# Queries and keys loaded on both halves of the partitions, and a step of its own for the store of x, in a kernel of block-causal attention, Fourier mixing and feed-forward

## The chip, the core and the metric

The kernel runs on one core of one Trainium2 chip. A core has five engines that work side by side and meet through semaphores: TensorE (PE; its weight loads are shown as PEld), VectorE (DVE), ScalarE (ACT), GpSimd (POOL) and SyncE (SP), which here only issues transfers. Each engine executes its own instructions in the order in which they were written; an instruction that waits holds up everything behind it on the same engine. Transfers run on 16 DMA engines. Data lies in SBUF, on 128 partitions; PE writes to PSUM. The metric is the time of one execution in microseconds, and lower is better.

## The reference

```python
# q, k, v: (8, 8, 576, 64), i.e. batch, heads, sequence, head dimension
scores = np.matmul(q, k.transpose(0, 1, 3, 2)) / np.sqrt(D)
mask = block_i >= block_j                      # blocks of 64 positions
attn = softmax(np.where(mask, scores, -1e9))   # in float32
x = np.matmul(attn, v)                         # put together to (8, 576, 512)
mixed = np.real(fft(fft(x, axis=1), axis=2))
u = x + mixed
un = (u - mean(u)) / np.sqrt(var(u) + 1e-6)    # over the last axis
out = u + np.maximum(un @ w_ch1, 0.0) @ w_ch2  # 512 -> 2048 -> 512
```

There are 8 batches of 8 heads, so 64 heads in all, numbered 0 to 63 here. All of it is asked for in float32.

## The kernel before

**One loop writes the whole order.** The kernel is cut into steps (the class Step, line 144): a function that writes instructions, its time on PE, a chain of later costs ("D0.95" is 0.95 us on DVE, "A" is ACT, "G" is POOL, "Q" is the DMA queue of SP, "L" is a latency that takes no engine), the keys it comes after, and a place. Lanes of steps (lines 363 to 502 and 904) each yield their steps in order. The loop at line 914 keeps a clock of its own by these costs: it issues, among the steps at the head of the lanes, the one with the lowest place that is due by that clock, and where none is due it puts in a step of the feed-forward matmuls (the filler) or of the preparation of the weights. So the order on each engine is fixed before the kernel runs, from estimates. Matmuls are kept in that order (line 202); the scheduler of the language below it may still shift instructions of the other engines against each other.

**One head.** Queries and keys come as one array of 64 rows (the head dimension) by 1152 columns (576 of q, then 576 of k). load_head (line 311) loads them to raw. A score is to have nearly float32 accuracy from matmuls in a format of fewer bits (fp32r), so q and k are each split into a leading part and a rest, and three of the four products are added up in PSUM. lead (line 316) rounds both on ACT (a cast of 64 x 1152) into LEAD, on partitions 0 to 63; below these, four rows hold the mask. REST (128 partitions) takes four quarters: in its q columns the rest of q on partitions 0 to 63 and a copy of the lead of q on 64 to 127; in its k columns a copy of the lead of k on 0 to 63 and the rest of k on 64 to 127. The two copies are transfers inside SBUF (lead_copies, line 319, lines 321 and 322), the rests are differences, one on DVE (line 328), one on POOL (line 330). So one matmul of REST with itself gives q_rest k_lead + q_lead k_rest, one of LEAD with itself q_lead k_lead and the mask (lines 404 and 405).

Each score group of a head (three groups of rows, n = 0, 1, 2; the first has four matmul pairs, the others one) goes from PSUM through the maximum (DVE, line 411), two exponentials (ACT, line 425, in f16 and f32), their difference (POOL, line 426), and a transpose by DMA from SP's queue (turn, line 430). PE then multiplies with V (values, line 435), and DVE divides by the sum (lines 463 to 467) into the tile x, which holds a pair of heads in one buffer. After the second head of a pair two transfers on SP's queue write x to a buffer in HBM (lines 471 and 474); they are written right behind the division, in the same step as the value matmuls.

LEAD, REST, raw and the probabilities have two buffers each, so head h reuses those of head h - 2. The planner lets the cast of head h start when the exponentials of head h - 2 are due (line 373), the scores when the copies (key TC, line 375) and both differences (T2) are due (line 483).

**After eight heads** a batch's x is read back from HBM in two orders (mirror, line 517, due when the last values of the batch are), transformed by matmuls, normalized, and fed to the feed-forward matmuls. Only batch 0 runs beside the loading and splitting of the weights (lines 793 to 876); heads of later batches are let in when the loading steps are written (line 922).

## Time and profile before

| what | value |
|---|---|
| time, median of 3 runs | 1315.21 us (1314.83 to 1320.55) |
| the profiled execution | 1318.01 us, its span 1316.2 us |
| mean granted clock of PE in it | 0.966 |
| instructions of PE, DVE, ACT, POOL | 9620, 1697, 1329, 715 |
| DMA traffic | 161.77 MB, mean 123 GB/s |
| transposes on SP's queue | 192 (three for each head) |

The profiled execution is one execution, taken by the hardware profiler. The span runs from its first instruction to its last. Views of it are used as follows: the page gives the busy time of each engine and its share of the span; the stretches give the same for parts of the span; the waits say which engine stood idle at which line and what ended that wait, summed up; the time order lists single instructions with start and duration; the groups put instructions of the same line, operation and shape together. A wait that hung on several semaphores is put down to the one that came last by the profile, which can be the wrong one.

### The profile page before, as it was taken

How to read it: one execution, taken by the hardware profiler on the slowest of the kernel's cores; microseconds unless marked ns; L12 is line 12 of the kernel's file. 1: busy time of each engine (PE TensorE's matmuls, PEld its weight loads, DVE VectorE, ACT ScalarE, POOL GpSimd, SP SyncE). 2: the span in 40 equal slices, each digit the busy share in tenths (PEclk: the TensorE clock that was granted, in tenths of full speed). 3: DMA queues.
4: the chain of work that ended last, by engine and by line, in shares of the span. 5: the costliest groups of instructions: out<-in, count | busy, mean ns of one | idle time of the engine just before them, and what ended most of it. 6: DMA issues, size and time to landing. Idle time of an engine off the chain costs nothing.

```text
span 1316.2 us, 25240 instructions
## 1 busy us (share of the span) xinstructions
PE 1125.2 (85%) x9620; PEld 826.4 (63%) x9620; DVE 713.2 (54%) x1697; ACT 620.6 (47%) x1329; POOL 549.0 (42%) x715
## 2 busy tenths in 40 slices
PE   1344175798989898989999999999999999999998
PEld 1244154575767676667767677667667767767665
DVE  7954477646465755576656656674673432412211
ACT  3645747764456543655666545665562211111110
POOL 2635725554455553536655366645741500300000
PEclk9999986798999998999999999999999999999999
DMA  9999607987568745765898567985863000000000
GB/s 320 230 203 237 176 5 141 163 172 151 96 148 152 172 85 130 144 152 116 173 193 165 108 120 191 173 167 114 172 119 82 26 16 17 21 1 17 16 17 16
DMA packets 307178, 161.77 MB, mean 123 GB/s; under 512 B 259281, under 2 KB 277857, under 8 KB 306929
## 3 DMA queue, kind: packets, MB, share of 16 engines
q1 hardware_dynamic: 300416, 135.94, 51.1%
q10 hardware_dynamic: 4384, 16.78, 3.9%
q0 software_dynamic: 2256, 7.45, 1.8%
q8 instruction: 75, 1.23, 0.4%
q14 instruction: 47, 0.38, 0.1%
HBM read 58.37 MB, written 18.87 MB: 59 GB/s over the span
## 4 chain that ended last, share of the span: by engine, by line
PE 52%; DVE 9%; DMA 8%; POOL 3%; issue 3%; ACT 2%; SPq 0%; DVEq 0%; POOLq 0%; ACTq 0%
PE h L202 20%; PE acc L202 20%; PE ps L202 8%; DMA turn<-prob 6%; PE av L202 3%; DVE M L411 2%; DMA u<-xd,rows 1%; DVE rest L328 1%; DVE tmp L541 1%; POOL prob L426 1%; PE ps L205 1%; ACT prob L425 1%; POOL rest L330 1%; ACT p L425 1%; DVE tmp L542 1%
## 5 line engine op out<-in xcount | busy, mean ns | idle before, releaser
L202 PE MATMUL h<-uh,W 128*128 128x256 f16 x2304 | 424.7, 276 | 0.0
L426 POOL TENSOR_TENSOR prob<-p,prob 128x288 f16<-128x288 f32 (+4 forms) x384 | 286.9, 754 | 276.2 <-ACT p L425 259.4
L202 PEld LDWEIGHTS <-W 128*128 128x128 f16 x3456 | 332.9, 99 | 67.1 <-issue 4.7
L202 PE MATMUL acc<-W,gh 128*128 128x512 f16 x1152 | 348.4, 384 | 0.0
L202 PE MATMUL h<-ul,W 128*128 128x256 f16 x1152 | 317.5, 276 | 0.0
L425 ACT ACTIVATE prob<-ps,M 128x64 f16<-128x64 f32 (+2 forms) x358 | 164.6, 493 | 138.6 <-DVE M L416 137.3
L742 DVE SCALAR_TENSOR_TENSOR gl<-h,gh 128x512 f16<-128x512 f32 x144 | 99.0, 687 | 238.6 <-ACT gh L741 238.2
L202 PE MATMUL acc<-W,gl 128*128 128x512 f16 x576 | 220.7, 383 | 1.1 <-DVE gl L742 0.6
L202 PE MATMUL av<-VH,turn 128*128 128x65 f16 x1920 | 130.7, 205 | 96.9 <-DMA turn<-prob 82.2
L741 ACT ACTIVATE gh<-h 128x512 f16<-128x512 f32 x144 | 86.7, 602 | 269.0 <-PE h L202 268.4
L202 PEld LDWEIGHTS <-turn 128*128 128x128 f16 x2880 | 116.9, 105 | 126.0 <-DMA turn<-prob 98.7
L411 DVE TENSOR_REDUCE M<-ps 128x1 f32<-128x288 f32 (+2 forms) x358 | 138.8, 426 | 88.1 <-PE ps L202 72.5
L425 ACT ACTIVATE p<-ps,M 128x64 f32<-128x64 f32 (+2 forms) x358 | 171.1, 494 | 15.1 <-POOL prob L426 12.5
L202 PEld LDWEIGHTS <-gh 128*128 128x128 f16 x1152 | 105.7, 100 | 97.1 <-issue 9.9
L330 POOL TENSOR_TENSOR rest<-raw,lead 64x576 fp32r<-64x576 f32 x64 | 106.9, 1671 | 115.7 <-ACT lead L317 89.4
L202 PE MATMUL ps<-rest 128*128 128x288 f32 (+2 forms) x358 | 123.7, 363 | 34.2 <-ACT p L425 26.6
L202 PE MATMUL av<-VL,turn 128*128 128x64 f16 x960 | 118.6, 204 | 0.0
L202 PEld LDWEIGHTS ps<-rest 128*128 128x128 f32 x358 | 73.8, 206 | 47.2 <-ACT p L425 32.3
L202 PE MATMUL ps<-lead 68*128 68x288 f32 (+2 forms) x358 | 103.3, 322 | 0.0
L202 PEld LDWEIGHTS <-gl 128*128 128x128 f16 x576 | 56.9, 99 | 71.5 <-issue 2.7
L317 ACT CAST lead<-raw 64x1152 fp32r<-64x1152 f32 x64 | 73.5, 1149 | 18.6 <-PE ps L202 18.4
L202 PEld LDWEIGHTS ps<-lead 68*128 68x128 f32 x358 | 74.3, 208 | 1.3
(166 smaller groups left out, 1197.2 us busy)
## 6 DMA issues: line engine op xcount, KB each, us to landing
raw<-in_qk_dram SPq DMA_DIRECT2D x64, 288.0 KB
rest<-lead SPq DMA_DIRECT2D x128, 144.0 KB
W<-in_moe_w_ch_dram ACTq DMA_DIRECT2D x14, 1024.0 KB
V<-in_v_dram SPq DMA_DIRECT2D x32, 320.0 KB
xd<-x SPq DMA_DIRECT2D x32, 256.0 KB
out_dram<-u SPq DMA_DIRECT2D x32, 256.0 KB
u<-xd SPq DMA_DIRECT2D x8, 512.0 KB
turn<-prob SPq DMA_TRANSPOSE x192
```

The source lines that it names most:

```text
L202: return tc.keep_in_program_order(nc.tensor.matmul(*args, **kw))
L205: return tc.keep_in_program_order(nc.tensor.transpose(*args, **kw))
L317: nc.scalar.copy(LEAD[h % NB][0:D, 64:], raws[h])
L328: nc.vector.tensor_tensor(x0[0:D, 64:64 + S], raw[:, 0:S], x1[0:D, 64:64 + S], op=ALU.subtract)
L330: nc.gpsimd.tensor_tensor(x0[D:P, 64 + S:], raw[:, S:], x1[0:D, 64 + S:], op=ALU.subtract)
L411: nc.vector.tensor_reduce(m[:, i:i + 1], x, axis=AX.X, op=ALU.max)
L425: nc.scalar.activation(to, x, AF.Exp, bias=bias[:, c:c + 1], scale=0.125)
L426: nc.gpsimd.tensor_tensor(pl, p32, ph, op=ALU.subtract)
L541: nc.vector.tensor_tensor(e[0:r], X[c][0:r], U[c][0:r], op=op)
L542: nc.vector.tensor_tensor(e[0:r, 1:256], e[0:r, 1:256], e[0:r, 511:256:-1], op=op)
L741: nc.scalar.activation(gh, t, AF.Relu)
L742: nc.vector.scalar_tensor_tensor(gl, t, 0.0, gh, op0=ALU.max, op1=ALU.subtract)
```

## The change

The array of queries and keys is doubled before the launch: its 64 rows come twice, so that raw has 128 partitions, both halves with the same data. The cast now fills all of ONE (the former REST): lead of q and of k on both halves. DVE then overwrites the q columns of the upper half with the rest of q, so ONE times ONE gives q_lead k_lead + q_rest k_lead. TWO (the former LEAD, with the mask rows) gets the lead of q by a new copy on DVE (lead_q, straight from raw into the fp32r tile) and the rest of k by POOL's difference; TWO times TWO gives q_lead k_rest and the mask. The two transfers inside SBUF are gone. In the planner the step that was "Q1.2", "L2.2" behind the cast is "D0.6" behind the load.

The two stores of a pair of x leave the values function and become store_x, issued by a lane of its own (store_lane) with place 2g + 1.6, due when the values of the pair are, with a cost of 1.1 us on SP's queue. The mirror of a batch now comes after the last of these steps, and the last value step of later heads asks for the store step of the pair before.

```diff
--- before.py
+++ after.py
@@ -229,8 +229,8 @@
 
 
     NB = 2
-    LEAD = [const.tile([KM, 64 + 2 * S], F32R, name=f"lead{i}") for i in range(NB)]
-    REST = [const.tile([P, 64 + 2 * S], F32R, name=f"rest{i}") for i in range(NB)]
+    TWO = [const.tile([KM, 64 + 2 * S], F32R, name=f"two{i}") for i in range(NB)]
+    ONE = [const.tile([P, 64 + 2 * S], F32R, name=f"one{i}") for i in range(NB)]
     PROB = [[const.tile([P, 2, w], F16, name=f"prob{i}_{x}") for i, w in enumerate(WIDTHS)] for x in range(2)]
     TURN = [const.tile([P, 2 * w // P, P], F16, name=f"turn{i}") for i, w in enumerate(WIDTHS)]
     DEN = [const.tile([P, 5], F32, name=f"DEN_{i}") for i in range(2)]
@@ -238,9 +238,9 @@
     VL = [const.tile([P, 5, 2, D], F16, name=f"VL_{i}") for i in range(2)]
     ZT = const.tile([34, NCOS], F32R, name="ZT")
     for i in range(NB):
-        nc.gpsimd.dma_start(LEAD[i][D:KM], c_masks)
-        nc.vector.tensor_scalar(LEAD[i][0:D, 0:64], ones[0:D, 0:64], 0.0, None, op0=ALU.mult)
-        nc.vector.tensor_scalar(REST[i][:, 0:64], ones[:, 0:64], 0.0, None, op0=ALU.mult)
+        nc.gpsimd.dma_start(TWO[i][D:KM], c_masks)
+        nc.vector.tensor_scalar(TWO[i][0:D, 0:64], ones[0:D, 0:64], 0.0, None, op0=ALU.mult)
+        nc.vector.tensor_scalar(ONE[i][:, 0:64], ones[:, 0:64], 0.0, None, op0=ALU.mult)
     for n, blocks in enumerate(BLOCKS):
         for j, at in blocks:
             for prob in PROB:
@@ -310,24 +310,24 @@
 
     def load_head(h):
 
-        raws[h] = work.tile([D, 2 * S], F32, name="raw", bufs=2)
+        raws[h] = work.tile([P, 2 * S], F32, name="raw", bufs=2)
         nc.sync.dma_start(raws[h], qk[h])
 
+
+
     def lead(h):
-        nc.scalar.copy(LEAD[h % NB][0:D, 64:], raws[h])
-
-    def lead_copies(h):
-        x0, x1 = REST[h % NB].bitcast(F32), LEAD[h % NB].bitcast(F32)
-        nc.sync.dma_start(x0[D:P, 64:64 + S], x1[0:D, 64:64 + S])
-        nc.sync.dma_start(x0[0:D, 64 + S:], x1[0:D, 64 + S:])
+        nc.scalar.copy(ONE[h % NB][:, 64:], raws[h])
+
+    def lead_q(h):
+        nc.vector.tensor_copy(TWO[h % NB][0:D, 64:64 + S], raws[h][0:D, 0:S])
 
     def rest(h, which):
 
-        x0, x1, raw = REST[h % NB], LEAD[h % NB].bitcast(F32), raws[h]
+        x, raw = ONE[h % NB].bitcast(F32), raws[h]
         if which == 0:
-            nc.vector.tensor_tensor(x0[0:D, 64:64 + S], raw[:, 0:S], x1[0:D, 64:64 + S], op=ALU.subtract)
+            nc.vector.tensor_tensor(ONE[h % NB][D:P, 64:64 + S], raw[D:P, 0:S], x[D:P, 64:64 + S], op=ALU.subtract)
         else:
-            nc.gpsimd.tensor_tensor(x0[D:P, 64 + S:], raw[:, S:], x1[0:D, 64 + S:], op=ALU.subtract)
+            nc.gpsimd.tensor_tensor(TWO[h % NB][0:D, 64 + S:], raw[0:D, S:], x[0:D, 64 + S:], op=ALU.subtract)
 
     def load_v(g):
         V = vraw[g] = work.tile([P, 5, 2, D], F32, name="V", bufs=1)
@@ -372,7 +372,7 @@
                 lambda: lead(h), 0.0, ("A1.15",), (("L", h),), ("T", h), place=h - 1.0,
                 need=(("E", h - NB, 2),) if h >= NB else (),
             )
-            yield Step(lambda: lead_copies(h), 0.0, ("Q1.2", "L2.2"), (("T", h),), ("TC", h), place=h - 0.9)
+            yield Step(lambda: lead_q(h), 0.0, ("D0.6",), (("L", h),), ("TC", h), place=h - 0.9)
             yield Step(lambda: rest(h, 0), 0.0, (_d(S),), (("T", h),), ("T2", h, 0), place=h - 0.8)
             yield Step(lambda: rest(h, 1), 0.0, (_g(S),), (("T", h),), ("T2", h, 1), place=h - 0.8)
 
@@ -390,7 +390,7 @@
 
     def scores(h, n):
 
-        x0, x1 = REST[h % NB], LEAD[h % NB]
+        x1, x2 = ONE[h % NB], TWO[h % NB]
         prob = PROB[h % 2][n]
         m = work.tile([P, 8], F32, name="M", bufs=2)
         found = {}
@@ -401,8 +401,8 @@
             for i, (j, lo, hi) in enumerate(parts):
                 q, k = slice(P * j, P * (j + 1)), slice(64 + S + lo, 64 + S + hi)
                 to = t[:, at:at + hi - lo]
-                mm(to, x0[:, q], x0[:, k], start=(i == 0), stop=False, skip_group_check=True)
-                mm(to, x1[:, q], x1[:, k], start=False, stop=(i == len(parts) - 1), skip_group_check=True)
+                mm(to, x1[:, q], x1[:, k], start=(i == 0), stop=False, skip_group_check=True)
+                mm(to, x2[:, q], x2[:, k], start=False, stop=(i == len(parts) - 1), skip_group_check=True)
                 places.append((j, lo, hi, to))
                 at += hi - lo
         chunks = [j for j, at in BLOCKS[n]]
@@ -466,12 +466,18 @@
         nc.vector.tensor_tensor(
             x[:, :, hh], av[:, :, 0:D], rec.unsqueeze(2).to_broadcast([P, 5, D]), op=ALU.mult
         )
-        if hh == 1:
-            ds = slice(D * (n - 1), D * (n + 1))
-            nc.sync.dma_start(
-                xd[64:576, ds].rearrange("(c p) d -> p c d", p=P), x[:, 1:5].rearrange("p c h d -> p c (h d)")
-            )
-            nc.sync.dma_start(xd[0:64, ds], x[64:128, 0].rearrange("p h d -> p (h d)"))
+
+    def store_x(g):
+        b, n = divmod(2 * g, H)
+        xd, x, ds = xs[b], xs["pair"], slice(D * n, D * (n + 2))
+        nc.sync.dma_start(
+            xd[64:576, ds].rearrange("(c p) d -> p c d", p=P), x[:, 1:5].rearrange("p c h d -> p c (h d)")
+        )
+        nc.sync.dma_start(xd[0:64, ds], x[64:128, 0].rearrange("p h d -> p (h d)"))
+
+    def store_lane():
+        for g in range(B * H // 2):
+            yield Step(lambda: store_x(g), 0.0, ("Q1.1", "L2.0"), (("V", 2 * g + 1, 2),), ("XS", g), place=2 * g + 1.6)
 
     def score_lane():
         for h in range(B * H):
@@ -498,7 +504,8 @@
                 yield Step(
                     lambda n=n: values(h, n), (0.75, 0.38, 0.29)[n], ("D0.95",) if n == 2 else (),
                     (("S", h, n), ("N", h // 2)) + ((("V", h - 1, 2),) if h else ()), ("V", h, n),
-                    need=(("d", h // H - 3, "u"),) if n == 2 and h >= 3 * H else (), place=h + 0.5,
+                    need=((("d", h // H - 3, "u"),) if n == 2 and h >= 3 * H else ()) + ((("XS", h // 2 - 1),) if n == 2 and h > 1 else ()),
+                    place=h + 0.5,
                 )
 
 
@@ -634,7 +641,7 @@
         D_ = lambda *a: ("d", b) + a
         place = H * (b + 0.9)
         yield Step(
-            mirror, 0.0, ("G3", "L2.5"), (("V", H * b + H - 1, 2),), D_("u"),
+            mirror, 0.0, ("G3", "L2.5"), (("XS", (H * b + H) // 2 - 1),), D_("u"),
             need=(("F", feed_number(b - 2, 1)),) if b > 1 else (), place=place,
         )
         for name, op, width in (("c", ALU.add, 257), ("s", ALU.subtract, 256)):
@@ -907,7 +914,7 @@
                 yield Step(load_tables, 0.0, ("G1",), (("V", 4, 2),))
             yield from fourier_steps(b)
 
-    lanes = [head_lane(), prepare_lane(), v_lane(), score_lane(), turn_lane(), value_lane(), transform_lane()]
+    lanes = [head_lane(), prepare_lane(), v_lane(), score_lane(), turn_lane(), value_lane(), store_lane(), transform_lane()]
     heads = [next(x) for x in lanes]
     weights, filler = weight_lane(), None
     side = next(weights)
@@ -965,6 +972,7 @@
 
 
     qk = np.stack([q, k], 2).reshape(B * H, 2, S, D).transpose(0, 3, 1, 2).reshape(B * H, D, 2 * S)
+    qk = np.concatenate([qk, qk], 1)
     v = v.reshape(B * H // 2, 2, S, D)
     vv = np.zeros((B * H // 2, P, 5, 2, D), v.dtype)
     vv[:, :, 1:5] = v[:, :, 64:576].reshape(-1, 2, 4, P, D).transpose(0, 3, 2, 1, 4)
```

## The prediction

> **What bounds the kernel now.** I read the page's head first, then the busy time of each engine by stage, then what TensorE waits for in two stages, then the DMA queue of SP, through which loads, copies, transposes and stores go in one order. Columns of the second fence: stretch, its length, busy us (and instructions) of PE, PEld, DVE, ACT and POOL, granted clock, DMA share, GB/s.
>
> ```profile
> span 1316.2 us, 25240 instructions
> PE 1125.2 (85%) x9620; PEld 826.4 (63%) x9620; DVE 713.2 (54%) x1697; ACT 620.6 (47%) x1329; POOL 549.0 (42%) x715
> ```
> ```profile
> 0.00:150.00 150.00, 53.55 (x468) 46.40 (x468) 91.99 (x197) 86.72 (x174) 75.69 (x101) 1.00 0.94 234
> 150.00:194.00 44.00, 21.77 (x102) 16.61 (x103) 33.03 (x70) 17.75 (x40) 14.65 (x22) 0.88 0.23 77
> 194.00:300.00 106.00, 83.16 (x779) 63.85 (x778) 67.33 (x178) 72.67 (x155) 58.78 (x65) 0.77 0.81 155
> 300.00:1045.00 745.00, 699.81 (x6424) 516.36 (x6422) 451.67 (x1132) 404.23 (x890) 382.45 (x498) 0.98 0.68 137
> 1045.00:1316.20 271.20, 266.93 (x1850) 183.19 (x1850) 69.15 (x122) 39.20 (x72) 17.44 (x31) 1.00 0.05 17
> ```
>
> PE is idle 191 us of 1316: 96.5 us before 150 (eight heads of batch 0 beside the loading of the weights), 22 us in the first Fourier stage, 23 us to 300, 45 us in the 745 us where the feed-forward matmuls fill each gap, 4 us at the end. The matmuls themselves don't change. So the change can only give or take idle time: at most 141 us lie before 300, 45 us behind it. What ends the idle time:
>
> ```profile
> PE av L202 <- DMA turn<-prob: 42.9, 15, 7.2
> PE ps L202 <- ACT tmp L343: 18.3, 1, 18.3
> ...
> PE av L202 <- DMA turn<-prob: 28.7, 24, 4.8
> PE ps L202 <- ACT p L425: 10.9, 8, 3.9
> PE ps L202 <- DMA rest<-lead: 1.3, 1, 1.3
> ```
> ```profile
> SPq L430 <- POOL prob L426: 156.5, 70, 9.5
> SPq L471 <- DVE x L466: 57.6, 12, 7.2
> ...
> SPq L321 <- ACT lead L317: 22.5, 6, 6.7
> ```
>
> The first two rows are PE's of 0 to 150, the next three of 300 to 1045 (us, times, longest), the last three SP's of 300 to 1045. PE waits for transposed probabilities, almost never for the copies by name (1.3 us). SP stands 22.5 us at the copies and 57.6 us at the stores of x, with transposes behind it; but mostly (156.5 us, 70 times) it waits at the transpose itself, for POOL's difference L426. A freer SP helps only where the difference was ready first.
>
> **The change part by part.** Costs of what is removed and of the neighbours of what is added (min/median/max ns):
>
> ```profile
> L317 ACT CAST lead<-raw x64: 1134/1151/1180, 10.5 to 972.9; 64x1152 fp32r<-64x1152 f32 x64
> L330 POOL TENSOR_TENSOR rest<-raw,lead x64: 1390/1663/2521, 11.8 to 974.2; 64x576 fp32r<-64x576 f32 x64
> L328 DVE TENSOR_TENSOR rest<-raw,lead x64: 737/752/1972, 16.2 to 974.7; 64x576 fp32r<-64x576 f32 x64
> ...
> L321 SPq DMA_DIRECT2D rest<-lead x64: 461/540/1194, 11.7 to 977.2; - x64
> L322 SPq DMA_DIRECT2D rest<-lead x64: 472/589/1427, 12.7 to 977.8; - x64
> ...
> L686 DVE TENSOR_SCALAR un<-u,ag x32: 517/542/1515, 184.6 to 1186.5; 128x512 f32<-128x512 f32 x32
> ```
>
> ```profile
> L509 ACT CAST fs<-tmp 128x257 fp32r<-128x257 f32 x16 | 6.4, 406 | 12.2 <-DVE tmp L542 12.1
> ...
> L548 ACT CAST fs<-tmp 32x257 fp32r<-32x257 f32 x8 | 3.2, 400 | 11.0 <-DVE tmp L542 11.0
> ```
>
> *Unchanged.* The cast covers 128 partitions where it covered 64. By the groups by shape (busy us, mean ns) a cast of ACT over 257 columns takes 406 ns on 128 partitions and 400 on 32, so it stays at 1.15 us. The two differences keep their shapes and engines, PE its matmuls.
>
> *The copies go.* 64 x (0.54 + 0.59) = 72 us of SP issue and their landings. At the start they gate scores:
>
> ```profile
> 23.74 0.60 SPq L322 DMA_DIRECT2D rest<-lead  x1
> ...
> 24.17 1.95 DVE L328 TENSOR_TENSOR rest<-raw,lead 64x576 fp32r<-64x576 f32 x1
> ...
> 31.07 0.58 PE L202 MATMUL acc<-rest 128*128 128x288 f32 x1 [7.98 <-DVE W L830]
> ...
> 40.00:50.00 10.00, 3.53 (x33) 2.99 (x31) 10.00 (x19) 6.52 (x15) 6.23 (x5) 1.00 1.02 258
> ```
>
> Head 1's second copy is issued at 23.74, its DVE difference ends at 26.1, its scores start at 31.07. No score reads the W that the row names; what is late is the copy. Without it the scores could start near 27, 4 us sooner. But DVE, which must reduce them, is busy 10.00 us of 10 in 40 to 50 (the third engine of that row): what PE gains waits at DVE. I count -1 us for the start (bounds 0 and -4). Later the path is on SP:
>
> ```profile
> 116.78 1.27 POOL L426 TENSOR_TENSOR prob<-p,prob 128x64 f16<-128x64 f32 x2
> ...
> 119.36 1.13 SPq L321 DMA_DIRECT2D rest<-lead  x1
> 120.53 0.60 SPq L322 DMA_DIRECT2D rest<-lead  x1
> ...
> 122.57 5.88 SPq L430 DMA_TRANSPOSE turn<-prob  x1
> ```
>
> Head 6's difference is done at 118.05, its transpose goes out at 122.57, and 1.73 us between are two copies for a later head. Such a delay is on the path when PE has no filler. For heads 4 to 16 I count -4 us (two like this one, a few at half; bounds 0 and 13 x 1.13 = -15), and -3 us behind 300, where PE's 28.7 us for transposes is the cap.
>
> *DMA.* The copies leave, a second half of raw comes: 288 KB of each per head.
>
> ```profile
> 458.00:458.25 0.25, 1.00 0.90 204
> 954.00:954.50 0.50, 1.00 0.89 295
> ```
>
> The first stretch holds copies alone, the second raw alone (share, GB/s). 295 KB at 204/0.90 = 227 GB/s take 1.3 us of all engines, at 295/0.89 = 331 GB/s 0.9 us: -0.4 us per head. The engines are 94% taken before 150, so some of 8 x 0.4 counts: -1 us. One load lands later by the same 0.9 us at most; its cast mostly comes many us later.
>
> *The written order.* The planner lets scores start when the copies are due, 0.25 + 1.2 + 2.2 + 0.25 = 3.9 us behind the cast by its own numbers; now the latest input is POOL's difference, due after 0.25 + (0.19 + 0.00194 x 576) + 0.25 = 1.8 us. So in the order scores may stand up to 2.1 us earlier, ahead of the head before's last value matmuls. Behind 300, where filler runs, this gives nothing. Before it, two heads go round in turn: scores, exponentials, transposes, then the next scores into the same buffers. For 6 such rounds I count 0.7 us each: -4 us (bounds 0 and 12 x 2.1 = -25).
>
> ```profile
> L471 SPq DMA_DIRECT2D xd<-x x32: 364/418/1637, 74.9 to 1001.7; - x32
> L474 SPq DMA_DIRECT2D xd<-x x32: 497/508/1322, 75.5 to 1002.1; - x32
> ```
>
> *The stores of x* are issued by a step due when DVE's product is due, so SP stops standing at them. What its standing there costs the transposes behind it is within the -3 and -4 above. Both DMAs of a pair (0.42 + 0.51 us to issue, as before) come behind whatever SP is given until then, transposes of the next head among it, and the mirror of a batch waits for its last pair: 0 to +1 us, once, before the first Fourier stage; later mirrors have filler beside them. The next pair's product waits for the store as it did, since x has one buffer.
>
> *The new DVE copy*, 64x576 f32 to fp32r, isn't in the trace. Nearest rows: one input over 128x512 takes 0.54 us (L686), two inputs over 64x576 0.75 us (L328).
>
> ```profile
> L328 DVE TENSOR_TENSOR rest<-raw,lead 64x576 fp32r<-64x576 f32 x64 | 67.8, 1059 | 9.5 <-ACT lead L317 9.0
> ...
> 88.25 0.69 DVE L828 TENSOR_SCALAR W<-W 128x1024 int32<-128x1024 int32 x1 [7.95 <-DMA W<-in_moe_w_ch_dram]
> ```
>
> I take 0.6 us, nearest to L686; bounds 0.3 (half of it, if a copy without scalars runs faster) and 1.06 us, L328's mean with its waits. That is 38 us (20 to 68) more on DVE's 713. Behind 300 DVE is busy 61% and PE has filler, yet the copy stands ahead of maxima that PE's transposes hang on: +2 us (0 to +10). Up to 88, where DVE is full or waits for the weights that it frees buffers for (the second row), the copies of heads 1 to 5 lie on the path: 5 x 0.6 = +3, and with the rest to 300 +4 us (0 to +12).
>
> **A rule that speaks against it.** First the rows:
>
> ```profile
> 610.77 1.73 DVE L686 TENSOR_SCALAR un<-left,ag 128x512 f32<-128x512 f32 x1
> 610.82 1.40 POOL L330 TENSOR_TENSOR rest<-raw,lead 64x576 fp32r<-64x576 f32 x1
> ```
>
> The same operation that takes 0.54 us in the median took 1.73 us here, beside a POOL operation of 1.40 us that started with it. The Trainium skill, SBUF — State Buffer, section "Who interferes with whom", says that VectorE and GpSimd share one pair of SBUF ports, that a plain copy may take it whole, and that the second to come waits until the first is through. By that rule, and the trace agrees here, the new copy can stop POOL's differences or be stopped by them. The Trainium skill, VectorE: DVE Perf Modes, section "Mode 2×_2P", lets a one-source fp32 operation in SBUF run two elements a cycle; as an estimate from that page the copy takes some 0.35 us and DVE's terms fall from +6 to +4.
>
> **The sum.** -1 - 4 - 3 - 1 - 4 + 1 + 4 + 2 = -6 us with the store's +1 at its worst, -7 without. The profiled execution took 1318.0 us, 1.8 beyond its span of 1316.2, and is 2.8 above the median of 1315.2; I carry the difference to the median: 1315.2 - 7 = 1308 us.
>
> **The rivals.**
> 1. *The start tightens* (1291 us). If each of 12 heads before 300 gains the whole 2.1 us of the order, that is -25 where the sum has -4 for the order and -4 for SP: 17 us more. For it: 96.5 + 23 us of idle time there. Against: DVE is busy 92 us of the first 150, DMA is 94% taken, and neither gets much less to do.
> 2. *Nothing to be measured* (1315 us). Gains are eaten by the DVE copy, or SP's standing only moves: the transposes still wait for POOL (156.5 us). For it: only 1.3 us of PE's waits behind 300 name a copy.
> 3. *Slower* (1325 us): the DVE copy collides with POOL's L426, whose end releases the transposes. Price from the rows above: 1.73 - 0.54 = 1.2 us a collision. One for every second of the 17 heads before 300 (10 us), and the 24 waits behind 300 longer by 0.3 us (7 us), come on top of the copy's own +6 and the store's +1, against gains of -13: about +10. It decides once the copy takes over 1.1 us in the mean, or L426 grows by 0.3 us a head.
>
> **How the numbers follow.** The forecast, 1301 to 1314 us with 1308 the likeliest, has 0.42; about half of it lies under 1308.6. Rival 1 has 0.14, rival 2 0.24, rival 3 0.20. About 0.5%, 6.6 us, is what a measurement of this kernel can tell from no change: faster means below 1308.6, slower above 1321.8. Faster: 0.24 + 0.14 and a part of rival 2's scatter, 0.42. Slower: rival 3's 0.20 and a little scatter of the order, 0.22. Same: 0.36. The range 1289 to 1326 leaves out half of rival 1 and the upper half of rival 3, under 0.2.
>
> **What would show it.** The first batch's attention ends with this store:
>
> ```profile
> 147.79 0.38 SPq L471 DMA_DIRECT2D xd<-x  x1
> ```
>
> Right: nothing but loads on SP between a POOL difference and its transpose; PE's waits for transposes below 42.9 us in the first 150 and 28.7 behind 300; this store some us before 147.79; the new copy at 0.4 to 0.8 us; DMA bytes unchanged. Wrong on the order: scores no closer behind the cast than now. Wrong on DVE: a copy of over 1.1 us, or L426 and L328 longer beside it. If the time to 300 stays and the rest moves, the gain was on SP, not in the start; if the start moves by tens of us, the written order did it, and the terms above are only its occasions.

## The result and the profile after

The changed kernel takes 1395.74 us (median of 4 runs, 1389.12 to 1402.51), the kernel before 1316.12 beside it (4 runs, 1314.83 to 1320.55): 1.0599 times as long, 95% interval 1.053 to 1.0668. The forecast was 1308 with a range of 1289 to 1326. The profiled execution of the changed kernel took 1402.51 us, the longest of its four. The head of its page, and its stretches (columns as before):

```profile
span 1400.7 us, 24983 instructions
PE 1156.0 (83%) x9620; PEld 847.4 (60%) x9620; DVE 795.0 (57%) x1761; ACT 625.2 (45%) x1329; POOL 547.7 (39%) x715
```
```profile
0.00:150.00 150.00, 48.91 (x421) 43.48 (x421) 103.05 (x200) 73.57 (x150) 66.16 (x91) 1.00 0.96 233
150.00:194.00 44.00, 16.65 (x106) 13.03 (x106) 25.52 (x49) 23.17 (x48) 17.64 (x16) 0.96 0.30 91
194.00:300.00 106.00, 79.89 (x676) 60.30 (x676) 71.39 (x172) 67.72 (x137) 53.52 (x63) 0.81 0.56 113
300.00:1045.00 745.00, 658.96 (x5942) 487.87 (x5943) 499.63 (x1167) 402.74 (x881) 375.47 (x487) 0.92 0.64 139
1045.00:1400.70 355.70, 351.57 (x2482) 242.68 (x2478) 95.42 (x176) 58.02 (x113) 34.95 (x58) 1.00 0.07 20
```

The instructions of PE are the same 9620. In the 745 us that PE's filler kept full before, it now stands for 86 us instead of 45, and does 5942 matmuls instead of 6424; the rest is pushed behind 1045. PE's waits of 0 to 150 (two rows), of 300 to 1045 (two rows), then SP's of 300 to 1045:

```profile
PE av L202 <- DMA turn<-prob: 48.9, 10, 13.2
PE ps L202 <- ACT tmp L343: 21.6, 2, 18.4
...
PE av L202 <- DMA turn<-prob: 61.6, 34, 5.5
PE ps L202 <- ACT p L425: 17.4, 14, 3.1
```
```profile
SPq L430 <- POOL prob L426: 179.4, 67, 9.4
SPq L314 <- DVE one L328: 63.0, 26, 9.1
SPq L473 <- DVE x L466: 53.6, 12, 9.7
```

PE waits more than twice as long for transposes behind 300. SP no longer stands at copies; it stands 63.0 us (6.5 before) at the load of a head, whose buffer DVE's difference L328 has yet to free, and at the stores of x (L473) nearly as long as before. The operations of the preparation, by line and then by group (busy us, mean ns, idle before):

```profile
L319 ACT CAST one<-raw x64: 1135/1152/1224, 10.8 to 1016.9; 128x1152 fp32r<-128x1152 f32 x64
...
L322 DVE CAST two<-raw x64: 410/442/1546, 14.8 to 1017.6; 64x576 fp32r<-64x576 f32 x64
```
```profile
L328 DVE TENSOR_TENSOR one<-raw,one 64x576 fp32r<-64x576 f32 x64 | 96.2, 1502 | 4.5 <-ACT one L319 2.3
L322 DVE CAST two<-raw 64x576 fp32r<-64x576 f32 x64 | 37.1, 580 | 0.0
```

The cast kept its 1.15 us and the new copy is as short as supposed, 0.44 us in the median. L328 went from a mean of 1059 ns to 1502.

That the copies are gone shows in the first heads. Head 1's scores began at 28.45 instead of 31.07 us, now behind VectorE's difference L328, and head 2's at 38.07 instead of 39.87. Then the gain is lost: head 0's three transposes lasted until 57.55 us instead of 48.46, and head 3's scores began at 80.47 instead of 71.15. PE's row of head 1 in the changed kernel, SP's row of the three transposes in it, and the same row of the kernel before:

```profile
28.45 0.61 PE L202 MATMUL acc<-one 128*128 128x288 f32 x1 [6.19 <-DVE one L328]
```
```profile
38.51 19.04 SPq L430 DMA_TRANSPOSE turn<-prob  x3
```
```profile
40.72 7.74 SPq L430 DMA_TRANSPOSE turn<-prob  x3
```

**Three parts of the time.** The two executions are best compared in three parts: the *start*, up to the first score matmul of head 8; the *heads*, from there to the end of the last product x; the *tail*, in which no head is left, only the Fourier stage of the last batch and feed-forward matmuls. The marks in the kernel before (time order, then L466 by line, whose last number is the start of the last one, 0.49 us long):

```profile
194.44 0.38 PE L202 MATMUL ps<-rest 128*128 128x288 f32 x1
```
```profile
L466 DVE TENSOR_TENSOR x<-av,rec x64: 456/491/493, 61.3 to 1001.2; 128x320 f32<-128x320 f32 x64
```

and in the changed kernel:

```profile
214.19 0.38 PE L202 MATMUL ps<-one 128*128 128x288 f32 x1
```
```profile
L466 DVE TENSOR_TENSOR x<-av,rec x64: 471/491/493, 75.3 to 1062.6; 128x320 f32<-128x320 f32 x64
```

So the start took 194.4 and now 214.2 us, the heads 807.2 and 848.9, the tail 314.6 and 337.6: +19.8, +41.7 and +23.0 make the 84.5 us between the spans. The same marks, read in each experiment's trace, give the table. The fifth column counts the matmuls that the written order leaves behind the last value matmul. Times and ratios are medians of the runs against the kernel before on the same chip; the parts are of one profiled execution. The times of one kernel differ by up to 18 us from run to run, and six kernels whose start is the same work in the same order (before, nudge_values, raw2_from_12, both twice_from_12 and copies_dve_cast) began head 8 at 188.5 to 196.6 us; so a difference of a few us between two parts says little.

| kernel | start | heads | tail | matmuls left | time | ratio, 95% |
|---|---|---|---|---|---|---|
| before | 194.4 | 807.2 | 314.6 | 2152 | 1316.12 | |
| after | 214.2 | 848.9 | 337.6 | 2319 | 1395.74 | 1.053 to 1.0668 |
| twice_old_order | 201.9 | 844.8 | 315.4 | 2152 | 1362.11 | 1.0278 to 1.0373 |
| copies_new_order | 202.4 | 829.4 | 337.6 | 2319 | 1372.58 | 1.0383 to 1.0475 |
| stores_only | 187.2 | 819.5 | 350.9 | 2409 | 1358.87 | 1.0294 to 1.0353 |
| twice_only | 210.8 | 844.7 | 331.1 | 2271 | 1382.06 | 1.0441 to 1.0525 |
| nudge_values | 193.7 | 808.0 | 331.1 | 2271 | 1334.18 | 1.0084 to 1.0192 |
| copies_dve | 196.1 | 857.7 | 314.6 | 2152 | 1371.58 | 1.0387 to 1.0495 |
| copies_raw2 | 228.3 | 811.6 | 314.5 | 2152 | 1352.87 | 1.0207 to 1.0338 |
| twice_old_act | 216.9 | 822.6 | 315.4 | 2152 | 1356.87 | 1.0252 to 1.0359 |
| raw2_from_12 | 188.5 | 813.6 | 314.6 | 2152 | 1319.32 | 1.0013 to 1.0057 |
| after_hop | 195.2 | 886.2 | 274.2 | 1834 | 1354.93 | 1.0223 to 1.0321 |
| before_hop | 186.9 | 850.5 | 286.5 | 1936 | 1319.86 | 0.9978 to 1.0032 |
| before_margin | 195.0 | 850.6 | 264.8 | 1825 | 1312.51 | 0.9944 to 0.9989 |
| twice_from_12_dve | 196.6 | 828.5 | 314.8 | 2152 | 1344.36 | 1.0188 to 1.0299 |
| twice_from_12_act | 192.0 | 819.4 | 314.8 | 2152 | 1328.02 | 1.0051 to 1.0111 |
| copies_dve_cast | 193.8 | 844.4 | 314.6 | 2152 | 1349.08 | 1.0214 to 1.0266 |
| after_act | 241.2 | 823.0 | 337.6 | 2319 | 1401.93 | 1.0613 to 1.0667 |
| after_from_12 | 202.3 | 844.9 | 337.6 | 2319 | 1381.02 | 1.0433 to 1.0513 |
| raw2_not_8_9 | 204.8 | 811.3 | 314.9 | 2152 | 1339.23 | 1.0139 to 1.0266 |

### The profile page after: what moved, and what is told of

It reads as the page before. It is cut to its first block, busy times and chain, and to the rows that moved or that the text cites. A ratio compares the mean times of both kernels' runs of the same rounds, so it can differ in the third digit from the quotient of the medians.

```text
span 1400.7 us, 24983 instructions
## 1 busy us (share of the span) xinstructions
PE 1156.0 (83%) x9620; PEld 847.4 (60%) x9620; DVE 795.0 (57%) x1761; ACT 625.2 (45%) x1329; POOL 547.7 (39%) x715
## 4 chain that ended last, share of the span: by engine, by line
PE 52%; DMA 15%; DVE 15%; POOL 6%; issue 6%; ACT 5%; SPq 1%; DVEq 0%; POOLq 0%; ACTq 0%
PE acc L202 21%; PE h L202 19%; DMA turn<-prob 12%; PE ps L202 7%; PE av L202 4%; DVE M L411 3%; POOL prob L426 3%; DVE one L328 2%; ACT prob L425 2%; DVE tmp L548 1%; ACT p L425 1%; POOL two L330 1%; DMA U<-xd,rows 1%; PE ps L205 1%; DVE W L836 1%
## 5 line engine op out<-in xcount | busy, mean ns | idle before, releaser
L426 POOL TENSOR_TENSOR prob<-p,prob 128x288 f16<-128x288 f32 (+4 forms) x384 | 288.7, 758 | 321.5 <-ACT p L425 312.6
L202 PE MATMUL acc<-W,gh 128*128 128x512 f16 x1152 | 355.9, 392 | 0.0
L425 ACT ACTIVATE prob<-ps,M 128x192 f16<-128x192 f32 (+3 forms) x357 | 164.2, 493 | 160.1 <-DVE M L416 159.6
L425 ACT ACTIVATE p<-ps,M 128x192 f32<-128x192 f32 (+2 forms) x357 | 170.4, 494 | 15.1 <-POOL prob L426 12.8
L411 DVE TENSOR_REDUCE M<-ps 128x1 f32<-128x64 f32 (+2 forms) x357 | 138.2, 426 | 59.4 <-PE ps L202 51.1
L330 POOL TENSOR_TENSOR two<-raw,one 64x576 fp32r<-64x576 f32 x64 | 101.7, 1589 | 121.9 <-ACT one L319 104.9
L202 PE MATMUL ps<-one 128*128 128x64 f32 (+2 forms) x357 | 128.8, 375 | 22.2 <-ACT p L425 20.5
L202 PE MATMUL ps<-two 68*128 68x64 f32 (+2 forms) x357 | 107.9, 336 | 0.0
L328 DVE TENSOR_TENSOR one<-raw,one 64x576 fp32r<-64x576 f32 x64 | 96.2, 1502 | 4.5 <-ACT one L319 2.3
L202 PEld LDWEIGHTS ps<-one 128*128 128x128 f32 x357 | 77.8, 218 | 34.5 <-ACT p L425 26.6
L319 ACT CAST one<-raw 128x1152 fp32r<-128x1152 f32 x64 | 73.8, 1153 | 26.6 <-PE ps L202 22.0
## 6 DMA issues: line engine op xcount, KB each, us to landing
W<-in_moe_w_ch_dram ACTq DMA_DIRECT2D x14, 1024.0 KB, 16.5
```

The source lines that it names most:

```text
L202: return tc.keep_in_program_order(nc.tensor.matmul(*args, **kw))
L319: nc.scalar.copy(ONE[h % NB][:, 64:], raws[h])
L328: nc.vector.tensor_tensor(ONE[h % NB][D:P, 64:64 + S], raw[D:P, 0:S], x[D:P, 64:64 + S], op=ALU.subtract)
L330: nc.gpsimd.tensor_tensor(TWO[h % NB][0:D, 64 + S:], raw[0:D, S:], x[0:D, 64 + S:], op=ALU.subtract)
L411: nc.vector.tensor_reduce(m[:, i:i + 1], x, axis=AX.X, op=ALU.max)
L425: nc.scalar.activation(to, x, AF.Exp, bias=bias[:, c:c + 1], scale=0.125)
```

## The experiments

**Data path and order apart.** The change touches two things: what a head's preparation does, and the costs by which the planner writes the order. Four kernels take them apart. twice_old_order has the new data path with the old costs and the old stores, so PE's order is that of before (in the traces, too, the 9620 matmuls of both stand in one sequence):

```diff
-            yield Step(lambda: lead_q(h), 0.0, ("D0.6",), (("L", h),), ("TC", h), place=h - 0.9)
+            yield Step(lambda: lead_q(h), 0.0, ("Q1.2", "L2.2"), (("T", h),), ("TC", h), place=h - 0.9)
```

> Queries and keys arrive twice, with the new copy on DVE, but its step keeps the due time of the copies in SBUF and the stores of x stand as before, so that PE's order is that of the kernel before. If the written order is the loss (theory ORDER): 1316 us, within 10. If the copy on DVE and what it collides with is the loss (theory DVE): 1370 us or more. Half and half: about 1350.

copies_new_order is its mirror: transfers inside SBUF as before, but planned by the new line, and the store lane; PE's order is that of the changed kernel, matmul by matmul.

```diff
-            yield Step(lambda: lead_copies(h), 0.0, ("Q1.2", "L2.2"), (("T", h),), ("TC", h), place=h - 0.9)
+            yield Step(lambda: lead_copies(h), 0.0, ("D0.6",), (("L", h),), ("TC", h), place=h - 0.9)
```

> The copies inside SBUF as before, nothing new on DVE, but planned with the due times of the changed kernel and with the step for the stores, so that PE's order is that of the changed kernel. ORDER: 1385 us or more, as the changed kernel. DVE: 1316 to 1325 us.

stores_only is the kernel before with the store lane alone, twice_only the changed kernel without it:

```diff
-    lanes = [head_lane(), prepare_lane(), v_lane(), score_lane(), turn_lane(), value_lane(), transform_lane()]
+    lanes = [head_lane(), prepare_lane(), v_lane(), score_lane(), turn_lane(), value_lane(), store_lane(), transform_lane()]
```

> The kernel before with the step of its own for the stores of x alone. If the stores are the loss (theory STORES): 1370 us or more. ORDER, where any other order costs alike: 1340 us or more. DVE: 1316 us, within 10.

> The changed kernel with the stores of x put back into the values step. STORES: 1316 us, within 10. DVE: 1385 us or more. ORDER: somewhere between 1330 and 1400, since the order is a third one.

Measured: 1362.11, 1372.58, 1358.87 and 1382.06 us. Each part alone costs 3 to 5%, and together they cost less than their sum: the new data path costs 44 us in the old order (1362.11 against 1317.72 of the kernel before beside it) and 23 in the new one (1395.74 against 1372.58). So neither of the single causes holds alone. The parts in the table say more: with the old order the tail is that of before, with the new order it is 337.6 with either data path. The stores' lane loses 36.3 us in the tail and 12.3 in the heads, and gains 7.2 in the start, with the same instructions in another order.

**Is it this order, or any order?** nudge_values changes nothing but one planned cost, by 0.05 us:

```diff
-                    lambda n=n: values(h, n), (0.75, 0.38, 0.29)[n], ("D0.95",) if n == 2 else (),
+                    lambda n=n: values(h, n), (0.75, 0.38, 0.29)[n], ("D1.0",) if n == 2 else (),
```

> The kernel before with nothing changed but the planned VectorE cost of the values step, 1.0 instead of 0.95 us. Every instruction is the same; the written order differs from the fourth batch of heads on. FITTED ORDER (the order of before is one that suits the chip better than its neighbours, and any other order that the planner writes costs some 40 us, as the three orders run so far did: +41 with the stores as a step, +55 with the copies, +34 with the data twice): 1345 to 1370, with less PE work between 300 and 1045 us than the 699.81 us of before. THESE STEPS (the orders run so far cost because the copies fell due earlier, or because the stores were a step of their own): 1310 to 1325.

1334.18 us, below the range of the one theory and above that of the other. PE's order parts from that of before at 242.5 us already, not only from the fourth batch of heads on as expected. Start and heads take what they took before; the order leaves 2271 matmuls for the end instead of 2152, and the tail is 16.5 us longer:

```profile
L466 DVE TENSOR_TENSOR x<-av,rec x64: 462/491/493, 61.3 to 1001.2; 128x320 f32<-128x320 f32 x64
```

119 matmuls for 16.5 us are 0.14 us each; the 257 of stores_only cost 36.3, the same. So 0.05 us more in the plan moved the time by 1.4%.

**Can a shorter tail be had?** after_hop, before_hop and before_margin change one constant of the planner each, after_hop on the changed kernel, the others on the kernel before:

```diff
-HOP = 0.25
+HOP = 0.5
...
-MARGIN = 0.3
+MARGIN = 1.0
```

> The changed kernel with the planner's HOP 0.5 instead of 0.25 us, so only its written order differs. Its order has 1834 matmuls behind the last values, where the changed kernel has 2319 and the kernel before 2152; the time behind the last x went with that number so far (2152: 314.6 us, 2271: 331, 2319: 337.7, 2409: 350.9, so 0.141 us each). TAIL (what an order leaves for the end is paid in full, the feed-forward matmuls fit into the idle time of PE before): tail 269 us and 1325 to 1345. TRADE (more feed-forward matmuls between the heads push the heads back by as much): 1385 to 1405 with the same tail.

> The kernel before with HOP 0.5 instead of 0.25 us: only the order differs, with 1936 matmuls behind the last values instead of 2152. TAIL: tail 284 us and 1280 to 1295, faster than both kernels. TRADE: tail 284 us as well, the heads longer by as much, 1310 to 1325. FITTED ORDER (the order of before suits the chip and any other loses): 1335 to 1370.

> The kernel before with MARGIN 1.0 instead of 0.3 us (a step of the heads must have been due for longer before it goes ahead of a feed-forward step): only the order differs, with 1825 matmuls behind the last values instead of 2152. TAIL: tail 268 us and 1268 to 1285. TRADE: tail 268 us and the heads longer by some 45 us, 1310 to 1325. FITTED ORDER: 1335 to 1370.

On the kernel before, TRADE holds: what the tail loses (28.1 and 49.8 us) the heads take (43.3 and 43.4), and with the start the times stay within 0.5%. before_margin is the one kernel faster than both, 1312.51 us, ratio 0.9967: less than 0.5%. after_hop gained 41 us on the changed kernel, less than TAIL said and far more than TRADE: 63.4 us of the tail and 19.0 of the start, against 37.3 in the heads. A short tail is a gain only where the heads don't pay for it.

**What the data path costs in the start.** copies_raw2 is the kernel before, order and copies included, with the load doubled and its upper half read by nobody. raw2_from_12 doubles it from head 12 on:

```diff
-        raws[h] = work.tile([D, 2 * S], F32, name="raw", bufs=2)
-        nc.sync.dma_start(raws[h], qk[h])
+        raws[h] = work.tile([P, 2 * S], F32, name="raw", bufs=2)
+        n = P if h >= 12 else D
+        nc.sync.dma_start(raws[h][0:n], qk[h][0:n])
```

> The kernel before with its copies and its order, and with queries and keys loaded on both halves of the partitions, the upper half read by nobody. LOAD (589,824 bytes instead of 294,912 for each head, landing later and in the way of transposes): 1345 to 1365. DVE OPERATION or SP: 1312 to 1322.

> As copies_raw2 (copies and order of before, queries and keys loaded on both halves), but heads 0 to 11, whose loads are issued beside the 14 weight loads of the start, load only the lower half. START (the doubled load costs only where the weight loads fill the DMA engines: in copies_raw2 head 8's scores began at 228.26 instead of 194.44 us, and from there to the last x it took 811.60 us against 807.19): head 8 starts at 193 to 197 again and the time is 1313 to 1324. LOAD EVERYWHERE (the doubled load delays transposes of every head): 1335 to 1350.

copies_raw2 took 1352.87 us, raw2_from_12 1319.32. The doubled load costs the heads 4 to 6 us, but the start 33.8, and nothing there once the first twelve heads load one half (the rows are head 8's first score matmul, of the first and the second kernel):

```profile
228.26 0.38 PE L202 MATMUL ps<-rest 128*128 128x288 f32 x1
```
```profile
188.54 0.38 PE L202 MATMUL ps<-rest 128*128 128x288 f32 x1
```

The time order of copies_raw2 shows where it goes (SP's rows, then one of POOL), and the rows of the kernel before for the same three transposes and the same load of POOL's queue follow:

```profile
102.56 0.52 SPq L314 DMA_DIRECT2D raw<-in_qk_dram  x1
103.19 51.38 SPq L430 DMA_TRANSPOSE turn<-prob  x3
```
```profile
103.69 0.59 POOL L902 DMA_DIRECT2D dft<-in_c_dft_dram  x1 [1.18 <-DVE dft L901]
```
```profile
108.42 10.89 SPq L430 DMA_TRANSPOSE turn<-prob  x3
```
```profile
109.53 0.59 POOL L902 DMA_DIRECT2D dft<-in_c_dft_dram  x1 [1.10 <-DVE dft L901]
```

Head 5's transposes met the load of the 2.6 MB of tables, and took 51.38 us instead of 10.89. But in the kernel before they meet the same load as closely, so the meeting alone isn't the cause. raw2_not_8_9 halves only the two loads that went out just before:

```diff
-        n = P if h >= 12 else D
+        n = D if h in (8, 9) else P
```

> As copies_raw2 (copies and order of before, doubled loads), but heads 8 and 9 load only the lower half. In copies_raw2 their loads went out at 100.66 and 102.56 us, the transposes of head 5 at 103.19, the 2.6 MB of the tables (L902, POOL's queue) at 103.69, and the three transposes took 51.38 us instead of 10.89. COLLISION (the start lost there what doubled loads right before these transposes and the tables cost): head 8's scores begin at 190 to 202 and the time is 1312 to 1328, though ten of the first twelve loads are doubled. BYTES (the start loses by the bytes that go beside the weight loads): 215 or later, 1340 to 1352.

1339.23 us, between the two ranges, with runs from 1332.75 to 1350.64. In the profiled execution, the fastest of the four, the three transposes took 26.50 us and head 8 began at 204.8. So a part of the start's loss hangs on these two loads and a part does not; bytes and collision can't be told apart further by these runs.

after_from_12 asks the same of the changed kernel: its own order, but heads 0 to 11 prepared as before.

```diff
+        n = D if h < 12 else P
+        nc.sync.dma_start(raws[h][0:n], qk[h][0:n])
...
+        if h < 12:
+            nc.scalar.copy(TWO[h % NB][0:D, 64:], raws[h][0:D])
+        else:
+            nc.scalar.copy(ONE[h % NB][:, 64:], raws[h])
```

> The changed kernel with its own order and stores, but heads 0 to 11 prepared as before (half a load, copies inside SBUF). SEPARATE PRICES (the start pays the doubled load, the heads the VectorE copy, the tail the order): head 8 starts at 193 to 203 instead of 214.2 us, the heads take 835 to 850, the tail 337.6, together 1370 to 1388. ORDER IN THE START (copies_new_order, with half loads in this order, began head 8 at 202.4, so the order keeps a part of the start): 203 or later, with 1380 to 1395.

```profile
202.26 0.38 PE L202 MATMUL ps<-one 128*128 128x288 f32 x1
```

The start ends at 202.3, at the edge of the two expectations and as in copies_new_order (202.4): of the 19.8 us, 11.9 belong to the new preparation of the first twelve heads and 7.9 to the order. What it is in the preparation stays open. In the six kernels that have it from head 0 on, head 3's scores began at 78.7 to 83.4 us, in all others at 65.7 to 75.6, and among these are copies_raw2 with the doubled load alone (65.7) and copies_dve with a VectorE copy alone (66.9). The time, 1381.02, lies where the two ranges overlap.

**What the data path costs in the heads.** Three kernels in the old order move or add the VectorE operation. twice_old_act runs the new copy on ScalarE; copies_dve is the kernel before with a copy of the load that nobody reads:

```diff
-        nc.vector.tensor_copy(TWO[h % NB][0:D, 64:64 + S], raws[h][0:D, 0:S])
+        nc.scalar.copy(TWO[h % NB][0:D, 64:64 + S], raws[h][0:D, 0:S])
...
+        nc.vector.tensor_copy(raws[h][D:P, 0:S].bitcast(F32R), raws[h][0:D, 0:S])
```

> Data twice, stores and order as before, as in twice_old_order (1362.11), but the new copy of the queries runs on ScalarE instead of VectorE. DVE OPERATION: most of the +44 goes, 1320 to 1335, the rest being 64 copies of some 0.7 us on ScalarE. LOAD or SP (the load of the next head but one stands at the differences with the transposes behind it): it stays, 1350 to 1370.

> The kernel before with its copies inside SBUF and its order, and beside them one VectorE copy of 64 x 576 for each head whose result nobody reads. DVE OPERATION (the new VectorE copy of 0.44 us and what it does to the operations behind it and to POOL beside it is the price of the data path, +44 in the old order): 1345 to 1365, with L328 well above its 1059 ns. LOAD or SP (the price is in the doubled load, or in where SP stands): 1315 to 1325, a few us for 64 x 0.44 = 28 us of an engine that is 54% busy.

twice_old_act came out at 1356.87, as the theory against the VectorE operation had it, and yet the parts speak for it in some measure: the heads lost 22.2 us less than in twice_old_order (822.6 against 844.8), and the start 15.0 more. A time that stays can be two changes that cancel. copies_dve took 1371.58, more than any theory said, and for another reason (groups of its profile):

```profile
L329 DVE TENSOR_TENSOR rest<-raw,lead 64x576 fp32r<-64x576 f32 x64 | 65.2, 1019 | 4.6 <-ACT lead L317 4.6
...
L323 DVE CAST raw<-raw 64x576 fp32r<-64x576 f32 x64 | 35.8, 559 | 115.4 <-DMA raw<-in_qk_dram 112.4 <-POOL prob L427 2.5
```

Its L329 (L328 of before) is no longer than before; VectorE stood 115.4 us at the added copy, 112.4 of them for the load. So it tells nothing of the operation, and copies_dve_cast repeats it with a copy made from the cast, from head 12 on:

```diff
+        if h >= 12:
+            nc.vector.tensor_copy(raws[h][D:P, 0:S].bitcast(F32R), x1[0:D, 64:64 + S])
```

> Order, copies and loads of before, and from head 12 on one more VectorE copy of 64 x 576 that nobody reads, made from the cast (as L328 is) and not from the load, so that VectorE needn't stand for the load as it did in copies_dve (89 us at L323). DVE OPERATION (0.45 us of VectorE at this place costs by itself): 1330 to 1350. STANDING (what copies_dve lost was the wait for the load, and in twice_old_order it is the place of L328 beside POOL's difference): 1314 to 1326.

```profile
L330 DVE TENSOR_TENSOR rest<-raw,lead 64x576 fp32r<-64x576 f32 x64 | 80.2, 1253 | 6.3 <-ACT lead L317 4.8
...
L324 DVE CAST raw<-lead 64x576 fp32r<-64x576 f32 x52 | 43.8, 842 | 6.7 <-ACT lead L317 3.6 <-POOL prob L428 1.7
```

1349.08 us, with 37.2 us more in the heads and nothing in start or tail. It stood for the load no more; the added copy (43.8 us) and a difference longer by 0.19 us are most of what VectorE had more to do, and in all it was busy for 763.2 us instead of 713.2. Of these 50.0 us the heads lose 37.2 in the profiled execution, the longest of four (the medians differ by 31.7), though nobody reads the copy and VectorE was idle 46% of the time before.

twice_from_12_dve and twice_from_12_act are twice_old_order and twice_old_act with heads 0 to 11 prepared as before (the edit of after_from_12), and after_act is the changed kernel with the copy on ScalarE:

> Order and stores of before. Heads 0 to 11 are prepared as before (half a load, copies inside SBUF); from head 12 on the data comes twice with the new copy on VectorE. SEPARATE PRICES (twice_old_order's 45.9 us of span are 7.4 of the start and 37.6 of the heads, the load paying in the start and the operations of the preparation behind it): head 8 starts at 187 to 198, the heads take 835 to 848 us, the time is 1338 to 1355. START ALONE (without the late start the heads would take what they take in before): 1313 to 1325.

> The same with the new copy on ScalarE. DVE OPERATION (the copy of 0.54 us and the longer L328 behind it, 1.54 instead of 1.26 us, are what VectorE loses for each head, and the heads took 844.8 us with it on VectorE and 822.6 on ScalarE): 15 to 25 us less than twice_from_12_dve, 1318 to 1335. DATA PATH (the heads lose by the load, the missing copies or where SP stands, wherever the copy runs): within 8 us of twice_from_12_dve.

> The changed kernel with its order and the new copy of the queries on ScalarE instead of VectorE. DVE OPERATION: the heads take some 827 us instead of 848.9, the tail stays 337.6, 1370 to 1385. DATA PATH or ORDER: 1390 to 1403.

1344.36 and 1328.02 us: against 1317.39 of the kernel before beside them the new data path, kept out of the start, still costs 27 us with the copy on VectorE and 11 with it on ScalarE. The heads took 828.5 (below the 835 to 848 expected) and 819.4. So with starts nearly alike (196.6 and 192.0) ScalarE made the heads 9.1 us shorter and the time 16.3, less than the 22.2 us of the heads in the pair above, whose starts differ by 15.0. after_act's heads took 823.0 instead of 848.9, as the theory of the operation had it (827), but its time stayed at 1401.93: its start grew to 241.2, where three transposes issued at 115.06 us, beside the load of the tables, took 41.22 us. So 25.9 us less in the heads stand beside 27.0 more in the start, and aren't the operation's price alone. L328 in the old order, 300 to 1045, with the copy on VectorE (twice_old_order) and on ScalarE (twice_old_act):

```profile
L328 DVE TENSOR_TENSOR one<-raw,one 64x576 fp32r<-64x576 f32 x46 | 70.8, 1540 | 2.2 <-ACT one L319 0.6
```
```profile
L328 DVE TENSOR_TENSOR one<-raw,one 64x576 fp32r<-64x576 f32 x47 | 59.1, 1258 | 5.4 <-ACT one L319 4.1
```

So the copy costs VectorE its own 0.54 us there and 0.28 us more at the difference behind it. What that difference waits for, the time order of the changed kernel shows (DVE, then POOL):

```profile
310.77 3.77 DVE L328 TENSOR_TENSOR one<-raw,one 64x576 fp32r<-64x576 f32 x1
314.57 0.49 DVE L466 TENSOR_TENSOR x<-av,rec 128x320 f32<-128x320 f32 x1
314.98 0.45 DVE L411 TENSOR_REDUCE M<-ps 128x1 f32<-128x288 f32 x1
```
```profile
310.77 1.40 POOL L330 TENSOR_TENSOR two<-raw,one 64x576 fp32r<-64x576 f32 x1 [3.74 <-ACT one L319]
312.13 1.79 POOL L426 TENSOR_TENSOR prob<-p,prob 128x448 f16<-128x448 f32 x2
```

L328, which takes 0.755 us at the least, begins with POOL's difference and ends 0.6 us behind the last of three POOL operations; the maximum L411 that the next exponentials need stands behind it. It is so for all 64 of the changed kernel: the 16 beside which GpSimd made no such difference took 0.755 or 0.756 us, the 14 that met one 1.25 us in the mean, the 28 that met two 1.71, the 6 that met three 3.13 (a longer one also meets more, so the 16 say most). The Trainium skill, SBUF — State Buffer, section "Who interferes with whom", has it that a VectorE operation with two inputs in SBUF and a GpSimd operation that reads SBUF share a read port; the trace agrees, with these numbers.

## Why the prediction was wrong

Its side was wrong, and 1395.74 lies 70 us beyond the range. By its steps:

1. *Unchanged.* "So the change can only give or take idle time" was wrong at the outset: PE's matmuls are the same 9620, but they were busy 30.8 us longer (1156.0 instead of 1125.2), and only 53.7 of the 84.5 us are idle time. The cast was right (1.152 us). "The two differences keep their shapes and engines" was right and not enough: the same L328 grew from 1059 to 1502 ns.
2. *The copies go*, -8 us: the gain was there in the first heads (head 1's scores 2.6 us sooner, where up to 4 were seen) and lost by head 3 (9.3 us later); the store that ends the first batch's attention went out at 154.28, not some us before 147.79. Later, SP only stands at another place (63.0 us at L314), and with the copies gone from head 12 on and the new operation on ScalarE the heads still took 12.2 us more than with the copies (twice_from_12_act).
3. *DMA*, -1 us: the wrong sign. The engines' time was counted, not what a load delays. The new preparation of the first twelve heads costs the changed kernel 11.9 us of start, and the doubled load alone cost copies_raw2 33.8 in the start.
4. *The written order*, -4 us, bounds 0 to -25: this step failed most. With nothing but the order and the stores' step changed, copies_new_order took 1372.58 us. The prediction followed one due time to the scores near it, as if the rest of the order stayed. The order is written anew from there on: 167 more matmuls were left for the end (23.0 us) and the start lost 7.9. With the copies kept, the heads of the new order took 22.2 us more as well. The prediction's last sentence, that a start moved by tens of us would be the order's doing, holds for 7.9 of 19.8.
5. *The stores of x*, 0 to +1 us, "so SP stops standing at them": it stands there still (53.6 us against 57.6), and alone the step cost 41 us (1358.87 against 1317.72), 36.3 of the span in the tail.
6. *The new DVE copy*, +6 us: its duration was right (0.44 us in the median, 0.58 in the mean; 0.6 was taken; the other estimate of 0.35 is below the shortest, 0.41). What it costs was not: run on ScalarE instead, it took 16.3 us less with the start as before (twice_from_12), and a VectorE copy that nobody reads cost 31.7 (copies_dve_cast). "Behind 300 DVE is busy 61% and PE has filler" was the step that fell: the share of idle time was taken for cover.
7. *Rival 3* had the side and the port, but the wrong victim. Neither of its two points was reached: the copy took 0.58 us in the mean, and L426 went from 754 to 758 ns. VectorE's L328 waits for POOL, not POOL for VectorE.

Adding up for the changed kernel, one step at a time, by the parts in the table: the new order with the stores' step (from the kernel before to copies_new_order) takes 8.0 us in the start, 22.2 in the heads and 23.0 in the tail; the new data path from head 12 on (from there to after_from_12) 15.5 in the heads and 0.1 less in the start; the new preparation of the first twelve heads (from there to the changed kernel) 11.9 in the start and 4.0 in the heads. That is 53.2 for the order and 31.3 for the data path. The shares hang on which comes first: with the data path first (twice_old_order) it takes 45.9 and the order 38.6. By the medians the order costs 55 as the first step and 34 as the last. A part of the order's 22.2 us may belong to copies_new_order alone: it plans the copies ahead of the cast that they read, and between 300 and 1045 us SP stood 35.9 us at them for the cast instead of 22.5. How the data path's share in the heads divides among the VectorE operation, the doubled load and the place where SP stands is open.

## What to carry to other kernels

Where a planner writes the order from estimates, a change of one cost is a new order, and its price is not near the step changed: count what the new order leaves for the end before you argue from waits, and time the change under the old order first. An engine that is 57% busy is no cover for an operation that stands ahead of the one the chain needs; price it at its full time, with what GpSimd beside it does to the operations behind it. Compare stage by stage: in four of these kernels (twice_old_act, after_act, before_hop, before_margin) one part gave most of what another took.

## What was not expected of the hardware

- Three transposes beside the load of the tables can take 51.38 us (copies_raw2) or 41.22 (after_act) instead of 10.89. From 103 to 150 us the DMA engines of copies_raw2 moved less than half of what those of before did (the row of copies_raw2, then of before):

```profile
DMA packets 2418, 4.42 MB, mean 94 GB/s; under 512 B 1934, under 2 KB 1934, under 8 KB 2293
```
```profile
DMA packets 17366, 9.63 MB, mean 205 GB/s; under 512 B 14667, under 2 KB 16395, under 8 KB 17235
```

  In the kernel before the transposes and the tables were issued at 108.42 and 109.53 us, in raw2_from_12 at 102.08 and 103.15, and the transposes took 10.89 and 10.63: nearness in time is not enough for it, and what else it takes stays open.
- The same 9620 matmuls kept PE busy for 1156.0 us instead of 1125.2. Between 300 and 1045 us, where PE stood more, the granted clock was 0.92 instead of 0.98. Whether the longer standing lowered it isn't shown: in the first 150 us PE stood for some two thirds of the time in both kernels, and the granted clock was 1.00.
